# Row sums from the additions, squares on ScalarE in the first batch, and one power on GpSimd for the inverse root of every norm

## The chip, the cores and the metric

The kernel runs on one core of a Trainium2 chip. The core has five engines with queues of their own: TensorE (PE in the profile, its weight loads PEld), VectorE (DVE), ScalarE (ACT), GpSimd (POOL) and SyncE (SP), which here only issues transfers. Each engine works through its queue in order; engines wait for one another by semaphores. The metric is the device time of one execution in microseconds; the median of several runs is compared.

## The reference

Two stages. A sparse attention over four batches of 8 heads, 768 tokens and 64 channels, where each query sees the keys within 16 positions and 24 block summaries, gives `x` of 4 x 768 x 512. Then a Fourier mix with a two-layer network:

```python
X = np.fft.fft(x, axis=1)
X = np.fft.fft(X, axis=2)
mixed = np.real(X).astype(np.float32)
u = x + mixed
mu = np.mean(u, axis=-1, keepdims=True)
var = np.mean((u - mu) ** 2, axis=-1, keepdims=True)
un = (u - mu) / np.sqrt(var + 1e-06)
ch = np.maximum(un @ w_ch1, 0.0) @ w_ch2
return (u + ch).astype(np.float32)
```

The change concerns `mu`, `var` and the division by the root. `w_ch1` is 512 x 2048 and `w_ch2` 2048 x 512; they arrive as 64-bit floats and are converted on the chip. All arithmetic is in fp32.

## The kernel before

The four batches follow one another, and each goes through attention, Fourier mix, normalisation, hidden layer and output layer. The attention of the next batch, and in batch 0 the conversion of the weights, are interleaved with the dense layers of the present one. Inside a batch the 768 tokens form two halves of three tiles of 128 tokens (HT = 3); a tile has 128 partitions (tokens) and 512 columns (channels, DM).

`gen_fourier(b)` does the mix. Products with cosine and sine tables give `y` (L1333), which ACT copies out (L1338, L1339). For each half, and in it for each tile `t`, matmuls with a second table give `mx` in PSUM (L1372 and L1374 in batch 0, L1290 and L1292 after it), which DVE adds onto `x[:, t, :]`. The helper `tt` records each of its DVE operations as L582, and `gtt` each of its POOL operations as L585.

Then come the row statistics. In batch 0 DVE computes them from each tile of x with `bn_stats` (L1381) and `bn_aggr` (L1382), and turns them into minus the mean (L1394) and the variance plus 1e-6 (L1395). In batches 1 to 3 ACT makes two passes over x: a copy scaled by -1/512 that adds up the row into `minus` (L1386), and a square of x + minus that adds up into `var` (L1388); DVE then divides by 512 and adds 1e-6 (L1397). The output of these ACT passes goes to `un`, which is overwritten later.

For each half the inverse root of the three columns of `var` is made on DVE: a shift and a subtraction on the bits (L1398, L1400) and three Newton steps of three operations (L1403, one at L582, L1405). L1406 multiplies it by `minus` to give the shift z. `normalise` then writes `un` = x * y + z, on DVE (L1354) for even tiles and for the last tile of batch 0, on ACT (L1351) otherwise. There are eight norms, two in each batch. TensorE turns `un` tile by tile (`unt`, L1428; L1425 in the last batch), DVE and ACT copy it to `u` (L1429), and DVE forms sums of blocks of u (`_right_sums`), since the dense layers use products of seven block sums in place of eight products.

The hidden layer `gen_hidden` makes `hx`, `hy`, `hz` (L1460), and the output layer `o` (L1730, first half of batch 0) and `ox`, `oy`, `oz` (L1753).

What sets the order: a planner with costs for each operation places instructions in the engines' queues by readiness and priority. `drive` interleaves generators step by step; the mix runs at a priority raised by 600. In batch 0 several places are pinned by `tc.issue_after(mark)`, which puts an instruction behind the marked one in the plan:

- The mixing matmuls of a tile come behind those of the tile before; the additions of tiles 4 and 5 onto x come behind the scaling of the first half (`marks["un", 0]`).
- `marks["mx", 0]` is first the z of a half and then its last scaling on DVE. The conversion of the second and later blocks of weights (`gen_weights`: DVE L1171, ACT L1172, DVE L1184, ACT L1185, DVE L1187, L1189 and one at L582), and the key maxima (L692) behind the products `ss` of batch 1's group 1, wait for it.
- The turns `unt` of the first half come behind `sc` of batch 1's group 0 (L810), those of the second behind `av` of it (L851).
- Batch 1's group 0 has its products of exponentials with the mask `near` on POOL (L585).

Of the kernel before, what the change touches and what calls it, by code (L numbers as in the profile page):

```python
# [9 lines left out]
FP = mybir.dt.float32  # L10
I32 = mybir.dt.int32
U32 = mybir.dt.uint32
AF = mybir.ActivationFunctionType
ALU = mybir.AluOpType
AX = mybir.AxisListType

P = 128
# [479 lines left out]
def _main_program(ctx, tc, q, k, v, moe_w_ch1, moe_w_ch2, out):  # L497


    nc = tc.nc  # L500
    B, H, S, D = q.shape
    DM = H * D
# [11 lines left out]
    HT = NST // 2  # L514
# [5 lines left out]
    ADD, SUB = ALU.add, ALU.subtract  # L520
# [4 lines left out]
    cpool = ctx.enter_context(tc.tile_pool(name="cst", bufs=1))  # L525
    apool = ctx.enter_context(tc.tile_pool(name="attn", bufs=2))
    bpool = ctx.enter_context(tc.tile_pool(name="bat", bufs=1))
    spool = ctx.enter_context(tc.tile_pool(name="small", bufs=4))
# [12 lines left out]
    near = cpool.tile([P, 2, NB2, BLOCK], FP, name="near")  # L541
    sel = cpool.tile([4 * nb, 2, P], FP, name="sel")
    half_of = cpool.tile([P, 2], FP, name="half")
    rebias = cpool.tile([P, 1], FP, name="rebias")
    mirror = cpool.tile([P, 1], I32, name="mirror")
    rec = cpool.tile([P, B * NP, 2, NST], FP, name="rec")
# [23 lines left out]
    def bank(shape, name):  # L570
        return psum.tile(shape, FP, tag="bank", bufs=4, name=name)
# [9 lines left out]
    def tt(out, in0, in1, op):  # L581
        return nc.vector.tensor_tensor(out=out, in0=in0, in1=in1, op=op).ins  # L582

    def gtt(out, in0, in1, op):
        return nc.gpsimd.tensor_tensor(out=out, in0=in0, in1=in1, op=op).ins  # L585
# [698 lines left out]
    def mix_halves(ps, y, fm, xt, half):  # L1284

        Q = DM // 4
        e0, eo, e1, o1 = fm[:, 0:Q + 1], fm[:, Q + 1:3 * Q + 1], fm[:, 3 * Q + 1:4 * Q + 1], fm[:, 4 * Q + 1:5 * Q + 1]
        nc.tensor.matmul(ps[:, 0:HD + 1:2], y[:, 0], e0, start=True, stop=False, skip_group_check=True)  # L1290
        for out, g, table in ((ps[:, 0:DM:2], 1, eo), (ps[:, 1:HD:2], 2, e1), (ps[:, HD + 1:DM:2], 3, o1)):
            nc.tensor.matmul(out, y[:, g], table, start=False, stop=True, skip_group_check=True)  # L1292
        low, high = xt[:, 1:HD], xt[:, HD + 1:DM]
        tt(xt[:, 0:HD + 1], ps[:, 0:HD + 1], xt[:, 0:HD + 1], ADD)
        tt(high, ps[:, HD - 1:0:-1], high, ADD)
        tt(low, low, ps[:, HD + 1:DM], SUB if half else ADD)
        tt(high, high, ps[:, DM - 1:HD:-1], ADD if half else SUB)

    def gen_fourier(b):
        x = x_of[b]  # L1300
# [12 lines left out]
        if b > 1:  # L1313
            big = rooms[b]
            yt = bpool.tile([P, 7, 2, S2], FP, tag="u", name=f"yt_{b}").rearrange("p a k n -> p (a k n)")[:, 0:8 * S2]
            un = big[:, 0:NST * DM]
        else:
# [4 lines left out]
            yt, un = big[:, 0:8 * S2], big[:, 8 * S2:8 * S2 + NST * DM]  # L1322
        yt = yt.rearrange("p (r g s) -> p r g s", r=2, g=4)
        un = un.rearrange("p (t d) -> p t d", t=NST)
        ty, tr = yt[:, 0], yt[:, 1]
        for par in range(2):
            for g in range(4):
                ps = bank([P, F2 + 2], f"y_{b}_{par}_{g}")
                y = ps[:, par:par + F2 + 1]
# [16 lines left out]
        def normalise(half, *which):  # L1346
            y, shift = norms[half]
            for i in which or range(HT):
                t = HT * half + i
                if t % 2 and not (b == 0 and t == NST - 1):  # L1350
                    nc.scalar.activation(out=un[:, t, :], in_=x[:, t, :], func=AF.Identity, bias=shift[:, i:i + 1],  # L1351
                                         scale=y[:, i:i + 1])
                else:
                    marks["un", half] = nc.vector.tensor_scalar(out=un[:, t, :], in0=x[:, t, :], scalar1=y[:, i:i + 1],  # L1354
                                                            scalar2=shift[:, i:i + 1], op0=ALU.mult, op1=ADD).ins
        for half in range(2):
            stat = spool.tile([P, 2, HT], FP, tag="stat", name=f"stat_{b}_{half}")
            norm = spool.tile([P, 2, HT], FP, tag="norm", name=f"norm_{b}_{half}")
            minus, var = stat[:, 0], stat[:, 1]
            if b == 0:  # L1360
                both = spool.tile([P, HT, 2], FP, tag="both", bufs=2, name=f"both_{half}")
            for i in range(HT):
                t = HT * half + i
                cols = slice(P * i, P * (i + 1))
                if b:
                    mix_halves(bank([P, DM], f"mx_{b}_{t}"), yt[:, half, :, cols], fd, x[:, t, :], half)
                else:

                    ps = bank([P, 2, HD], f"mx_{b}_{t}")
                    with tc.issue_after(marks["tile"]) if t else ExitStack():  # L1370
                        for par in range(2):
                            nc.tensor.matmul(ps[:, par, :], yt[:, half, 2 * par, cols], fd[:, 3 * par, :],  # L1372
                                             start=True, stop=False)
                            ins = nc.tensor.matmul(ps[:, par, :], yt[:, half, 2 * par + 1, cols],  # L1374
                                                   fd[:, 3 * par + 1 + half, :], start=False, stop=True)
                    marks["tile"] = ins.ins
                    xv = x[:, t, :].rearrange("p (m two) -> p two m", two=2)
                    with tc.issue_after(marks["un", 0]) if t > HT else ExitStack():
                        tt(xv, ps, xv, ADD)
                    bst = spool.tile([P, 6], FP, tag="bst", name=f"bst_{b}_{t}")  # L1380
                    nc.vector.bn_stats(out=bst, in_=x[:, t, :])  # L1381
                    nc.vector.bn_aggr(out=both[:, i], in_=bst)  # L1382
                    yield
                    continue

                nc.scalar.activation(out=un[:, t, :], in_=x[:, t, :], func=AF.Copy, scale=-1.0 / DM,  # L1386
                                     accum_out=minus[:, i:i + 1])
                nc.scalar.activation(out=un[:, t, :], in_=x[:, t, :], func=AF.Square, bias=minus[:, i:i + 1],  # L1388
                                     accum_out=var[:, i:i + 1])
                yield  # L1390

            y, z = norm[:, 0], norm[:, 1]
            if b == 0:
                nc.vector.tensor_scalar(out=minus, in0=both[:, :, 0], scalar1=-1.0, scalar2=None, op0=ALU.mult)  # L1394
                nc.vector.tensor_scalar(out=var, in0=both[:, :, 1], scalar1=1e-6, scalar2=None, op0=ADD)  # L1395
            else:
                nc.vector.tensor_scalar(out=var, in0=var, scalar1=1.0 / DM, scalar2=1e-6, op0=ALU.mult, op1=ADD)  # L1397
            nc.vector.tensor_scalar(out=y.bitcast(I32), in0=var.bitcast(I32), scalar1=1, scalar2=None,  # L1398
                                    op0=ALU.arith_shift_right)
            nc.vector.tensor_scalar(out=y.bitcast(I32), in0=y.bitcast(I32), scalar1=-1.0, scalar2=float(0x5F3759DF),  # L1400
                                    op0=ALU.mult, op1=ADD)
            for _ in range(3):
                nc.vector.scalar_tensor_tensor(out=z, in0=y, scalar=-0.5, in1=y, op0=ALU.mult, op1=ALU.mult)  # L1403
                tt(z, z, var, ALU.mult)
                nc.vector.scalar_tensor_tensor(out=y, in0=z, scalar=1.5, in1=y, op0=ADD, op1=ALU.mult)  # L1405
            ins = nc.vector.tensor_tensor(out=z, in0=minus, in1=y, op=ALU.mult)  # L1406
            if b == 0:
                marks["mx", 0] = ins.ins
            norms.append((y, z))
            if b == 0:  # L1410
                normalise(half)
                marks["mx", 0] = marks["un", half]
# [4 lines left out]
        for t in range(NST):  # L1417
            half, i = divmod(t, HT)
            if b:
                normalise(half, i)  # L1420
            ps = bank([P, 2, 2, P], f"unt_{b}_{t}")
            with tc.issue_after(marks[("av", 1, 0) if half else ("sc", 1, 0)]) if b == 0 else ExitStack():
# [6 lines left out]
            ins = (nc.vector.tensor_copy if t % 2 and (b or half) else nc.scalar.copy)(  # L1429
                out=u[:, half:half + 3:2, :, P * i:P * (i + 1)], in_=ps)  # L1430
# [372 lines left out]
    ps = bank([P, 512], "warm")  # L1803
# [2 lines left out]
    nc.scalar.dma_start(out=wide, in_=dr["wide"].ap())  # L1806
    nc.scalar.dma_start(out=count, in_=dr["count"].ap())
    nc.scalar.dma_start(out=blk, in_=dr["blk"].ap())
    nc.vector.memset(rebias, -896.0 * 2.0 ** 23)
    for kt, km in zip(kt_bufs, km_bufs):  # L1810
        nc.vector.memset(kt[:, 0:W], 0.0)
# [6 lines left out]
    for vw in vw_bufs + [third]:  # L1818
        nc.gpsimd.tensor_copy(out=vw[:, :, D].rearrange("p (e n) -> p e n", e=2),
                              in_=count[:, None, :].to_broadcast([P, 2, NQ]))  # L1820
# [52 lines left out]
    for b in range(B):  # L1873
# [20 lines left out]
        if b == B - 2:  # L1894
# [9 lines left out]
            ps = bank([1, 1], "flag_ps")  # L1904
# [5 lines left out]
def kernel(tc, q, k, v, moe_w_ch1, moe_w_ch2, out):  # L1910
    nc = tc.nc
    with ExitStack() as ctx:
        flag = _main_program(ctx, tc, q, k, v, moe_w_ch1, moe_w_ch2, out)
        redo = nc.values_load(flag[0:1, 0:1], min_val=0, max_val=1)
    with tc.If(redo > 0):
        _general_program(tc, q, k, v, moe_w_ch1, moe_w_ch2, out)
# [30 lines left out]
```

## Time and profile before

| | us |
|---|---|
| median of 3 runs | 783.42 (783.32 to 783.82) |
| the profiled execution | 782.39 |
| its span in the trace | 780.6 |

The profile is of one execution. Its span leaves out 1.8 us around it. The clock granted to TensorE was 0.999 over the span. A row of the timeline gives start, length, engine, line, operation, output and inputs, and in brackets the idle time of the engine before it and what ended that. Rows that follow each other alike are merged (`x3`), and some operations overlap the one before, so lengths are not distances. "Busy" for PE has modelled ends.

### The profile page before, as it was taken

What the parts mean: (1) busy time and instruction counts of PE and PEld (TensorE: products, weight loads), DVE (VectorE), ACT (ScalarE), POOL (GpSimd) and SP (SyncE); (2) the same over time, 40 slices, a digit from 0 to 9 for tenths busy, and PEclk for the clock granted to TensorE, in tenths of its full rate; (3) what the DMA queues carried; (4) which work ended last, traced back from release to release, by engine and by line L of the source; (5) the groups of instructions that cost most, each with busy time, mean ns of one, the idle gap of its engine ahead of it and who ended that gap; (6) DMA issues with size and microseconds to landing.
All of it is one profiled execution on the core that took longest, in us unless ns stands there. A gap on an engine that the chain in (4) does not pass through costs nothing.

```text
span 780.6 us, 14876 instructions
## 1 busy us (share of the span) xinstructions
PE 766.1 (98%) x6020; PEld 578.0 (74%) x6020; DVE 534.4 (68%) x1123; ACT 249.4 (32%) x579; POOL 74.7 (10%) x102
## 2 busy tenths in 40 slices
PE   8999899999999999999999999999999999999997
PEld 5778555446598866787578866688669889889886
DVE  5789998777888556652758544553576887766762
ACT  4765656326536022100236012200126124104300
POOL 1001000000000030201210020300030004101500
PEclk9999999999999999999999999999999999999999
DMA  9998979696855179986342169720624143204001
GB/s 203 259 240 163 217 253 302 178 280 175 245 141 157 37 214 219 248 124 182 128 166 96 55 209 197 200 81 1 255 63 143 41 181 143 95 1 188 1 29 57
DMA packets 135900, 120.35 MB, mean 154 GB/s; under 512 B 94512, under 2 KB 117392, under 8 KB 135824
## 3 DMA queue, kind: packets, MB, share of 16 engines
q1 hardware_dynamic: 134672, 117.05, 54.9%
q0 software_dynamic: 576, 2.10, 0.7%
q8 instruction: 49, 0.80, 0.5%
q10 hardware_dynamic: 576, 0.17, 0.1%
q14 instruction: 27, 0.22, 0.1%
HBM read 95.71 MB, written 23.59 MB: 153 GB/s over the span
## 4 chain that ended last, share of the span: by engine, by line
PE 81%; DVE 9%; DMA 5%; ACT 3%; issue 1%; SPq 1%; POOL 0%; DVEq 0%; ACTq 0%; POOLq 0%
PE ox L1753 18%; PE hx L1460 13%; PE oz L1753 9%; PE hz L1460 6%; PE o L1730 5%; PE oy L1753 4%; PE t L1633 4%; DMA words<-in_moe_w_ch_dram 3%; PE hy L1460 3%; PE y L1333 2%; PE f L1633 2%; PE mx L1292 2%; PE sc L810 2%; PE av L846 1%; DVE w L582 1%
## 5 line engine op out<-in xcount | busy, mean ns | idle before, releaser
L1460 PE MATMUL hx<-u,w 128*128 128x384 f32 x384 | 140.0, 492 | 0.5 <-ACT h L1471 0.3
L1460 PEld LDWEIGHTS hx<-u,w 128*128 128x128 f32 x384 | 70.9, 190 | 52.8 <-ACT p L817 3.7
L1753 PE MATMUL oz<-w,s 128*128 128x256 f32 x336 | 81.7, 380 | 0.0
L1753 PE MATMUL ox<-w,s 128*128 128x256 f32 x336 | 80.1, 380 | 0.2 <-DVE s L582 0.2
L1753 PE MATMUL ox<-w,h 128*128 128x256 f32 x336 | 79.6, 381 | 0.0
L1753 PEld LDWEIGHTS ox<-w,h 128*128 128x128 f32 x336 | 63.0, 190 | 10.7 <-issue 1.2
L1460 PE MATMUL hz<-u,w 128*128 128x384 f32 x192 | 70.4, 487 | 0.4 <-DVE u L582 0.4
L582 DVE TENSOR_TENSOR x<-ox,x 128x256 f32<-128x256 f32 x84 | 35.5, 423 | 51.2 <-PE ox L1753 50.8
L1753 PEld LDWEIGHTS ox<-w,s 128*128 128x128 f32 x336 | 63.0, 190 | 9.6 <-DVE s L582 0.6
L1753 PEld LDWEIGHTS oz<-w,s 128*128 128x128 f32 x336 | 63.2, 190 | 9.0 <-DVE x L582 0.4
L1460 PEld LDWEIGHTS hz<-u,w 128*128 128x128 f32 x192 | 36.2, 190 | 25.7 <-DVE u L582 1.0
L1471 ACT COPY h<-hx 128x384 f32<-128x384 f32 x24 | 11.5, 478 | 118.7 <-PE hx L1460 118.7
L1730 PE MATMUL o<-w,h 128*128 128x512 f32 x96 | 42.2, 595 | 0.9 <-DVE w L582 0.9
L1753 PE MATMUL oy<-w,h 128*128 128x256 f32 x168 | 40.7, 381 | 0.7 <-ACT h L1682 0.7
L1636 ACT COPY f<-t 128x192 f32<-128x192 f32 x52 | 15.8, 303 | 78.3 <-PE t L1633 78.1
L1612 POOL TENSOR_SCALAR h<-h 128x768 f32<-128x768 f32 x12 | 25.4, 2128 | 137.6 <-DVE h L1592 137.6
L585 POOL TENSOR_TENSOR vb<-vb 96x512 f32<-96x512 f32 (+2 forms) x20 | 20.4, 1024 | 182.5 <-DMA vb<-in_v_dram 115.8
L1460 PE MATMUL hy<-u,w 128*128 128x384 f32 x96 | 35.2, 488 | 1.5 <-DVE h L582 1.5
L582 DVE TENSOR_TENSOR x<-oz,x 128x256 f32<-128x256 f32 x42 | 17.8, 423 | 26.7 <-PE oz L1753 26.4
L1753 PEld LDWEIGHTS oy<-w,h 128*128 128x128 f32 x168 | 31.5, 190 | 5.9 <-ACT h L1682 1.5
L1730 PEld LDWEIGHTS o<-w,h 128*128 128x128 f32 x96 | 18.0, 190 | 23.8 <-issue 21.2
L1490 ACT ACTIVATE h<-hx 128x384 f32<-128x384 f32 x24 | 11.7, 489 | 62.2 <-PE hx L1460 62.2
(236 smaller groups left out, 1327.4 us busy)
## 6 DMA issues: line engine op xcount, KB each, us to landing
w<-dw SPq DMA_DIRECT2D x42, 896.0 KB, 5.8
words<-in_moe_w_ch_dram SPq DMA_DIRECT2D x32, 512.0 KB, 5.8
dw<-w SPq DMA_DIRECT2D x12, 896.0 KB, 7.8
vw<-in_v_dram SPq DMA_DIRECT2D x47, 192.0 KB, 5.6
out_dram<-x SPq DMA_DIRECT2D x23, 256.0 KB, 2.0
vb<-in_v_dram SPq DMA_DIRECT2D x24, 192.0 KB, 6.9
kn<-in_k_dram SPq DMA_DIRECT2D x9, 384.0 KB, 5.9
qn<-in_q_dram SPq DMA_DIRECT2D x9, 384.0 KB, 7.0
```

The source lines that it names most:

```text
L582: return nc.vector.tensor_tensor(out=out, in0=in0, in1=in1, op=op).ins
L585: return nc.gpsimd.tensor_tensor(out=out, in0=in0, in1=in1, op=op).ins
L810: ins = nc.tensor.matmul(ps[h][r:r + 64, i, :], kt[rows, o:o + 64], qt[rows, o:o + BLOCK], start=True, stop=True)
L1292: nc.tensor.matmul(out, y[:, g], table, start=False, stop=True, skip_group_check=True)
L1333: nc.tensor.matmul(y, fgs[b][par][:, st, P * g:P * (g + 1)], fs[par][:, g % 2, st, :], start=(st == 0), stop=(st == n - 1))
L1460: ins = nc.tensor.matmul(ps, w[:, a, kk, :], u[:, r, kk, :], start=start and kk == 0, stop=stop and kk == 1, skip_group_check=True)
L1490: nc.scalar.activation(out=c21, in_=X, func=AF.Relu)
L1612: nc.gpsimd.tensor_scalar(out=t, in0=t, scalar1=0.0, scalar2=None, op0=ALU.max)
L1633: marks["two"] = nc.tensor.matmul(o, left(j, a, m), rhs(r, m), start=m in (1, 5), stop=m in (2, 3, 4, 5, 7), skip_group_check=True).ins
L1636: nc.scalar.copy(out={1: f[:, 0], 6: f[:, 1], 7: g}[m], in_=t)
L1730: nc.tensor.matmul(ps, h[:, n, hf, P * t:P * (t + 1)], wt[2, b, j][:, 2 * hf:2 * hf + 2, :], start=(n, hf) == (0, 0), stop=(n, hf) == (NC ...
L1753: nc.tensor.matmul(ps, left[a][:, n, :], wt[2, b, j][:, r, :], start=start and n == 0, stop=stop and n == NC - 1, skip_group_check=True)
```

## The change

In batch 0 the addition of `mx` onto x becomes a `scalar_tensor_tensor` that also adds up the row into `minus`, now the plain sum; ACT squares -512 x + sum and adds that up into `var`, which is therefore 512 to the third times the variance. `bn_stats`, `bn_aggr` and what followed them are gone. In every batch one DVE operation scales `var` and adds 1e-6, one POOL operation raises it to the power -0.5 (a constant tile `root`), and one DVE operation makes z. The shift, the subtraction and the Newton steps are gone.

```diff
+    root = cpool.tile([P, HT], FP, name="root")
...
-            if b == 0:
-                both = spool.tile([P, HT, 2], FP, tag="both", bufs=2, name=f"both_{half}")
...
                     with tc.issue_after(marks["un", 0]) if t > HT else ExitStack():
-                        tt(xv, ps, xv, ADD)
-                    bst = spool.tile([P, 6], FP, tag="bst", name=f"bst_{b}_{t}")
-                    nc.vector.bn_stats(out=bst, in_=x[:, t, :])
-                    nc.vector.bn_aggr(out=both[:, i], in_=bst)
+                        nc.vector.scalar_tensor_tensor(out=xv, in0=ps, scalar=1.0, in1=xv, op0=ALU.mult, op1=ADD,
+                                                       accum_out=minus[:, i:i + 1])
+                    nc.scalar.activation(out=un[:, t, :], in_=x[:, t, :], func=AF.Square, bias=minus[:, i:i + 1],
+                                         scale=-float(DM), accum_out=var[:, i:i + 1])
...
-            if b == 0:
-                nc.vector.tensor_scalar(out=minus, in0=both[:, :, 0], scalar1=-1.0, scalar2=None, op0=ALU.mult)
-                nc.vector.tensor_scalar(out=var, in0=both[:, :, 1], scalar1=1e-6, scalar2=None, op0=ADD)
-            else:
-                nc.vector.tensor_scalar(out=var, in0=var, scalar1=1.0 / DM, scalar2=1e-6, op0=ALU.mult, op1=ADD)
-            nc.vector.tensor_scalar(out=y.bitcast(I32), in0=var.bitcast(I32), scalar1=1, scalar2=None,
-                                    op0=ALU.arith_shift_right)
-            nc.vector.tensor_scalar(out=y.bitcast(I32), in0=y.bitcast(I32), scalar1=-1.0, scalar2=float(0x5F3759DF),
-                                    op0=ALU.mult, op1=ADD)
-            for _ in range(3):
-                nc.vector.scalar_tensor_tensor(out=z, in0=y, scalar=-0.5, in1=y, op0=ALU.mult, op1=ALU.mult)
-                tt(z, z, var, ALU.mult)
-                nc.vector.scalar_tensor_tensor(out=y, in0=z, scalar=1.5, in1=y, op0=ADD, op1=ALU.mult)
-            ins = nc.vector.tensor_tensor(out=z, in0=minus, in1=y, op=ALU.mult)
+            nc.vector.tensor_scalar(out=var, in0=var, scalar1=1.0 / DM ** (1 if b else 3), scalar2=1e-6, op0=ALU.mult, op1=ADD)
+            gtt(y, var, root, ALU.pow)
+            ins = nc.vector.scalar_tensor_tensor(out=z, in0=minus, scalar=1.0 if b else -1.0 / DM, in1=y, op0=ALU.mult,
+                                                 op1=ALU.mult)
...
+    nc.vector.memset(root, -0.5)
```

## The prediction

> **What bounds the kernel now.** I read the page's busy times first, then a table of busy times by stage, then what TensorE waited for, then the timeline around the first batch's normalisation.
>
> ```profile
> span 780.6 us, 14876 instructions
> ...
> PE 766.1 (98%) x6020; PEld 578.0 (74%) x6020; DVE 534.4 (68%) x1123; ACT 249.4 (32%) x579; POOL 74.7 (10%) x102
> ```
>
> TensorE (PE) is busy for 766.1 of 780.6 us. The change touches no matmul, so all that it can win is idle time of PE: 14.5 us in all, and only what lies behind a norm. The table by stage says where that is. Its columns are the stretch, its length, and the busy us of PE, weight loads, DVE, ACT and POOL.
>
> ```profile
> 60.00:65.00 5.00, 5.00 (x31) 4.51 (x30) 5.00 (x15) 3.19 (x7) 0.00 (x0) 1.00 1.41 165
> 65.00:70.00 5.00, 5.00 (x116) 4.34 (x115) 4.72 (x19) 2.30 (x5) 0.01 (x1) 1.00 1.11 292
> 70.00:75.00 5.00, 4.97 (x212) 3.81 (x210) 4.52 (x21) 3.11 (x8) 1.96 (x2) 1.00 0.40 99
> 75.00:80.00 5.00, 4.63 (x40) 3.12 (x40) 5.00 (x8) 4.94 (x9) 0.00 (x0) 1.00 0.02 3
> 80.00:85.00 5.00, 4.40 (x18) 2.43 (x19) 5.00 (x6) 4.29 (x10) 0.00 (x0) 1.00 0.86 230
> 90.00:100.00 10.00, 8.51 (x194) 5.36 (x194) 10.00 (x15) 3.48 (x5) 0.00 (x0) 1.00 1.19 232
> 224.00:262.00 38.00, 37.66 (x213) 33.66 (x213) 31.73 (x91) 16.44 (x47) 0.00 (x0) 1.00 0.43 118
> 402.00:432.00 30.00, 29.85 (x177) 27.19 (x176) 23.00 (x74) 17.08 (x47) 0.00 (x0) 1.00 0.32 108
> 582.00:613.00 31.00, 30.85 (x180) 27.78 (x179) 23.74 (x74) 17.09 (x47) 0.00 (x0) 1.00 0.33 107
> ```
>
> The last three rows are the mixing of batches 1 to 3, where six of the eight norms are: PE idles 0.34, 0.15 and 0.15 us there, so a faster norm can win 0.6 us at most. The six rows above are batch 0. There VectorE (DVE) is full from 75 on, and PE loses 0.37, 0.60 and 1.49 us. The list of PE's waits between 53 and 224 us names them:
>
> ```profile
> PE hy L1460 <- DVE h L582: 1.5, 1, 1.5
> PE o L1730 <- DVE w L582: 0.9, 1, 0.9
> ...
> PE hz L1460 <- DVE u L582: 0.4, 1, 0.4
> PE ss L828 <- DVE km L692: 0.4, 1, 0.4
> ```
>
> So the stretch from 75 to 100 is bound by DVE with PE close behind, and the question is how much earlier DVE gets there. The timeline of batch 0 (start, length, engine, line, operation):
>
> ```profile
> 61.55 0.67 DVE L582 TENSOR_TENSOR x<-mx,x 128x512 f32<-128x512 f32 x1
> ...
> 67.25 0.59 PE L1374 MATMUL mx<-fd,big 128*128 128x256 f32 x2
> ...
> 67.91 0.16 DVE L1406 TENSOR_TENSOR norm<-stat,norm 128x3 f32<-128x3 f32 x1
> ...
> 69.31 1.53 PE L1428 MATMUL unt<-ident,big 128*128 128x128 f32 x12
> ...
> 69.99 1.97 POOL L585 TENSOR_TENSOR p<-p,near 128x384 f32<-128x384 f32 x2 [30.05 <-ACT p L817]
> ...
> 72.09 0.17 DVE L1398 TENSOR_SCALAR norm<-stat 128x3 int32<-128x3 int32 x1
> ...
> 74.27 0.16 DVE L1406 TENSOR_TENSOR norm<-stat,norm 128x3 f32<-128x3 f32 x1
> ...
> 74.47 1.00 DVE L1354 TENSOR_SCALAR big<-x,norm 128x512 f32<-128x512 f32 x2
> ...
> 75.39 0.69 DVE L1171 TENSOR_SCALAR words<-words 128x1024 int32<-128x1024 int32 x1
> ...
> 75.80 1.53 PE L1428 MATMUL unt<-ident,big 128*128 128x128 f32 x12
> ```
>
> The second half's z (L1406) ends at 74.43 and its two scalings on DVE at 75.47. The weight conversion (L1171) begins at 75.39, since the code holds it, and the key maxima behind PE's ss, until that scaling is issued (the mark ("mx", 0)). From there DVE never rests until 100. The path is: last x of the half, its statistics, norm, scaling, conversions, then PE's waits.
>
> **The change part by part.** What DVE loses:
>
> ```profile
> L1381 DVE BATCH_NORM_STATS2 bst<-x 128x6 f32<-128x512 f32 x6 | 3.9, 682 | 0.0
> ...
> L1382 DVE BATCH_NORM_AGGREGATE both<-bst 128x2 f32<-128x6 f32 x6 | 0.8, 166 | 0.0
> ...
> L1394 DVE TENSOR_SCALAR stat<-both 128x3 f32<-128x3 f32 x2 | 0.4, 192 | 0.0
> ...
> L1405 DVE SCALAR_TENSOR_TENSOR norm<-norm 128x3 f32<-128x3 f32 x24 | 3.8, 156 | 0.4
> ```
>
> Batch 0 drops 3.9 + 0.8 + 0.4 us of statistics. Each of the eight norms drops eleven small operations. Bare, as in the second half, they follow each other at 0.20 us (72.09 to 74.27 for the eleven steps to L1406), so 2.2 us. In batches 1 to 3 other work of DVE and PE lies over them, and PE had at most 0.6 us to give; I count nothing. If a norm came late there, u would have to be late: batch 1's last sum ends at 258.9 and the first hidden product runs at 272.28, so some 13 us cover it.
>
> ```profile
> 257.97 0.95 DVE L582 TENSOR_TENSOR u<-u 128x768 f32<-128x768 f32 x1
> ...
> 272.28 1.29 PE hx L1460 x4
> ```
>
> What is added. First, six additions become a form that also sums the row. The addition is 0.67; the read-out of a sum is not in DVE's rows. I bound it by nothing and by ACT's read-out, 0.19, and take 0.19: it stands between x and the square. Second, ACT gets six squares in batch 0:
>
> ```profile
> L1388 ACT ACTIVATE big<-x,stat 128x512 f32<-128x512 f32 x6 | 4.3, 717 | 0.1
> ...
> L1388 ACT ACTIVATION_READ_ACCUMULATOR big<-x,stat 128x1 f32 x6 | 1.1, 187 | 0.0
> ...
> L585 POOL TENSOR_TENSOR fold<-fold 128x1 f32<-128x1 f32 x4 | 0.8, 192 | 0.3
> ...
> L585 POOL TENSOR_TENSOR fold<-fold 1x1 f32<-1x1 f32 x4 | 1.1, 278 | 0.3
> ```
>
> That is 0.72 + 0.19 = 0.91 each and 5.5 us together, in a stretch (60 to 75) where ACT is busy for 8.6 of 15 us. Third, the power on POOL. No row shows one. Below stands a two-input addition of one column, 0.19; above, eleven small POOL operations, as many as it replaces on DVE, at 0.28: 3.1 us. I take 0.5, near the small addition, as three columns are little data. Each hand-over between engines I count at 0.1 (POOL started at 69.99, on the first ACT result of a pair begun at 69.41 with some half a microsecond each). A VectorE operation that awaits the last one costs 0.2.
>
> Half 0: x of tile 2 ends at 62.22, with its sum at 62.4; square to 63.3, variance to 63.5, power 63.6 to 64.1, z from 64.2 to 64.4, against 68.07. PE's turn of that half stands at 69.31 behind matmuls that the change doesn't touch, so nothing is won there directly. Half 1: the last mixing matmul ends at 67.84; x with its sum to 68.7, square 69.6, variance 69.8. If POOL is free, the power ends at 70.4 and z at 70.7. If the planner leaves the two products with near ahead (69.99 to 71.96), POOL is free only at 71.96 and z ends at 72.8. z was 74.43, so the **lead is 1.6 to 3.7 us**; I take 2.7. What is queued behind z on DVE are the scalings, conversions and key maxima: all gain the same lead. Behind the power on POOL only the near products can stand; half a microsecond later they end at 72.5, still before av uses them.
>
> What the lead is worth: PE's waits for ss (0.4), hz (0.4) and hy (1.5), 2.3 us. A lead of 1.6 takes 1.6 of it, one of 2.3 or more all. PE's next wait, o for w (0.9), hangs on a string of ACT work that begins when PE delivers hz, and moves along with PE; I count nothing for it, 0.9 as the upper end. PE is otherwise full, so nothing comes late in place of these. **Sum: -2.3 us** (bounds with the mechanism intact -1.6 and -2.3 - 0.9 = -3.2): span 778.3, and 782.39 - 2.3 = 780.1 for the profiled execution. The median of the runs is 783.42, 1.03 above that execution, so **781.1 us** as a median.
>
> [...]
>
> **The rivals.**
>
> (a) The lead is spent, not handed on. DVE's order is the planner's. The hy wait ended with an h addition at 96.44 that stood behind conversion work:
>
> ```profile
> 95.84 0.68 DVE L582 TENSOR_TENSOR w<-w 128x512 f32<-128x512 f32 x1
> ...
> 96.44 0.55 DVE L582 TENSOR_TENSOR h<-hy,h 128x384 f32<-128x384 f32 x1
> ```
>
> If the planner uses the lead to put more conversion in front of it, the 1.5 us stays and only the 0.8 of ss and hz is won: 782.6, no change that can be measured. For it: DVE is full, with conversions enough. ACT speaks for it too: it is busy for 9.2 of 10 us from 75 to 85, each conversion passes through it, and it now gets the squares before. Against it: the total of work before the addition is smaller.
>
> (b) Slower: the power itself. Let it take p. Above p = 2.3 half 0 delays the second half, for tiles 4 and 5 are added only behind the first half's scaling. From tile 2's x at 62.4 it is then 1.5 + p for half 0's z (square 0.9, variance 0.2, two hand-overs, z 0.2), 1.1 for the scalings, 1.4 for two additions with their sums, and again 1.5 + p: z of half 1 at 67.9 + 2p, and p = 3.3 eats the whole lead. At p = 5, z is at 77.9 instead of 74.43: the turn of half 1 and the conversions are 3.5 later, and the median is 786.9. Against it: POOL's addition of 384 columns takes 1.0 us (1.97 for two), so three columns would need to cost 1.6 us each. My upper bound of 3.1 stands just short of the point.
>
> [...]
>
> (c) More: the 0.9 of o goes as well, and PE's small waits on ACT and in batches 1 to 3: 2.3 + 0.9 + 0.6 = 3.8, 779.6.
>
> **How the numbers follow.** A measurement of this kernel tells about 0.2%, 1.6 us, from no change. The forecast (-1.6 to -3.2) gets 0.48, (c) 0.05, (a) with the start-up case 0.31, (b) 0.16, as p is unknown and the planner may place things badly. Faster 0.53, same 0.31, slower 0.16. The range goes from (c), 779.6, to 784.4: past (a) and the start-up case, leaving out most of (b).
>
> **What would show it.** Right: L1381, L1382 and the small operations gone; each power under 1 us on POOL; z of half 1 near 71 to 73 and the first conversion behind it by 74; the waits of ss, hz and hy shrunk; the table for batches 1 to 3 unchanged in PE. Wrong: the conversions early but hy still waiting (a); a POOL row of 3 us or more, with PE idle before the turn at 69 or 76 (b); squares standing behind the copies of kt and qt on ACT, so that half 0 gains nothing.

## The result, and the profile after

The changed kernel takes 787.61 us as a median (785.57 to 789.29), against 783.37 us for the kernel before in the same comparison. The ratio is 1.0054, with a 95% interval of 1.0036 to 1.0072: **slower by 4.2 us**, where 2.3 us less were forecast. The page of the changed kernel, in the lines that answer to those shown of before:

```profile
span 783.8 us, 14797 instructions
...
PE 768.5 (98%) x6020; PEld 581.7 (74%) x6020; DVE 523.0 (67%) x1028; ACT 253.1 (32%) x591; POOL 82.5 (11%) x110
...
PEclk9999899999999999999999999999999999999999
```

DVE lost 11.4 us of work, as meant. PE does the same 6020 matmuls and is busy for 2.4 us longer, and in the row of the granted clock one slice, the fifth (78 to 98 us), is no longer full. The norm itself went as forecast. The timeline of the second half of batch 0 (start, length, engine, line):

```profile
69.90 0.85 POOL L586 TENSOR_TENSOR norm<-stat,root 128x3 f32<-128x3 f32 x1 [5.69 <-DVE stat L1392]
...
70.72 0.99 POOL L586 TENSOR_TENSOR p<-p,near 128x384 f32<-128x384 f32 x1
...
70.78 0.95 DVE L1394 SCALAR_TENSOR_TENSOR norm<-stat,norm 128x3 f32<-128x3 f32 x1 [0.97 <-POOL norm L586]
...
72.69 0.69 DVE L1172 TENSOR_SCALAR words<-words 128x1024 int32<-128x1024 int32 x1
```

The power takes 0.85 us, z ends at 71.73 and the conversion starts at 72.69, against 74.43 and 75.39 before. The last mixing matmul ended 0.55 us earlier in this execution (67.29), so the lead is 2.15 us.

Then comes ScalarE (ACT). What stands further back in its queue waits for what stands ahead. Its timeline after the change, and below it before:

```profile
69.64 0.49 ACT L818 ACTIVATE p<-sc 128x384 f32<-128x384 f32 x1
71.77 0.81 ACT L1352 ACTIVATE big<-x,norm 128x512 f32<-128x512 f32 x1 [1.64 <-DVE norm L1394]
72.49 1.54 ACT L1418 COPY u<-unt 128x512 f32<-128x512 f32 x3
73.91 0.51 ACT L818 ACTIVATE p<-sc 128x384 f32<-128x384 f32 x1
74.29 0.51 ACT L830 ACTIVATE p<-ss 128x384 f32<-128x384 f32 x1
74.66 1.18 ACT L1173 ACTIVATE words<-words,rebias 128x1024 int32<-128x1024 int32 x1
...
76.64 0.54 ACT L837 ACTIVATE vs<-vs,half 128x64 f32<-128x64 f32 x2
```

```profile
69.41 0.88 ACT L817 ACTIVATE p<-sc 128x384 f32<-128x384 f32 x2 [0.42 <-PE sc L810]
70.27 1.56 ACT L1429 COPY u<-unt 128x512 f32<-128x512 f32 x3
71.71 0.52 ACT L829 ACTIVATE p<-ss 128x384 f32<-128x384 f32 x1
72.09 0.55 ACT L836 ACTIVATE vs<-vs,half 128x64 f32<-128x64 f32 x2
74.53 0.82 ACT L1351 ACTIVATE big<-x,norm 128x512 f32<-128x512 f32 x1 [1.89 <-DVE norm L1406]
```

Before, everything that batch 1's attention needs (two exponentials of sc, one of ss, the two vs copies) was done by 72.6, and un tile 3, which has to wait for z, stood behind it all. With the shorter norm the planner sets un tile 3 ahead of the second exponential. ACT then stands still for 1.64 us waiting for z, although the input of the second exponential (sc) had been ready since 68.83. That exponential, the one of ss and the vs copies start 2.6 to 4.6 us later than before. PE needs them. Its timeline:

```profile
71.36 1.23 PE L811 MATMUL sc<-qt,kt 64*64 64x32 f32 x34
74.47 1.59 PE L811 MATMUL sc<-qt,kt 64*64 64x32 f32 x62 [1.88 <-ACT p L818]
75.99 2.78 PE L847 MATMUL av<-vw,p 64*32 64x65 f32 x96
```

The sc matmuls stop for 1.88 us. The av matmuls after them take 2.78 us, where the same 96 took 1.55 before. The table by stage shows why (stretch, its length, busy us of PE, clock, DMA share, GB/s):

```profile
76.00:77.00 1.00, 1.00 (x46) 0.58 0.00 0
77.00:78.00 1.00, 1.00 (x44) 0.50 0.07 16
...
82.00:83.00 1.00, 1.00 (x6) 0.51 0.90 236
```

From 76.2 to 83.0 us TensorE is granted half its clock (0.50 in the rows of 77 to 82), which costs 3.4 us by an estimate, half of those 6.8. The profile is no exception in this: the mean clock over the span was 0.992 to 0.995 in all eight runs of the changed kernel. The list of PE's waits:

```profile
PE sc L811 <- ACT p L818: 1.9, 1, 1.9
PE hx L1449 <- ACT h L1460: 1.4, 2, 0.9
...
PE ox L1742 <- DVE x L583: 1.2, 3, 0.5
```

The waits of ss, hz and hy that were to go have gone. In their place stand the one of sc, more waiting of hx for ACT (1.4 us, where it was 0.3), and a new one of ox in the mixing of the later batches. Two such rows of batch 3:

```profile
604.08 1.57 PE L1414 MATMUL unt<-ident,fold 128*128 128x128 f32 x12 [0.31 <-DVE fold L1355]
...
609.13 0.70 PE L1742 MATMUL ox<-w,s 128*128 128x256 f32 x2 [0.45 <-DVE x L583]
```

The start of the program varies: the last mixing matmul of batch 0 ended between 66.8 and 70.5 us in the twelve profiles of this study. The clock divides them. In e3_power123, e4_exps_first, e6_values_first and e10_before_vs_late it was half for 3.4 us between 9.2 and 13.5 us, some 50 us ahead of the norm, and there the matmul ended at 69.0 to 70.5; in the other eight it stayed full there, and the matmul ended at 66.8 to 67.9. Runs of one kernel differ in the clock too: of 24 runs of the kernel before, the five fastest (781.6 to 782.01 us) had a mean clock of 0.999 or 1.0 and the five slowest (785.07 to 787.32) one of 0.994 to 0.996. So the kernels are compared from that matmul on. The table gives the length of five stages of TensorE's timeline: from the end of that matmul to the first hx, and on to the first mixing matmul of batches 1, 2 and 3 and the end of the last matmul. The first row is in us; the others are differences from it, each from one profile.

| kernel | to first hx | to batch 1 | to batch 2 | to batch 3 | to the end | sum |
|---|---|---|---|---|---|---|
| before | 11.00 | 153.28 | 176.97 | 180.68 | 186.07 | 708.00 |
| after | +5.92 | -3.15 | -0.66 | +0.91 | +0.81 | +3.83 |
| e1_squares | +6.39 | -1.65 | -0.56 | 0.00 | +0.01 | +4.19 |
| e2_power | +6.21 | -3.04 | +0.47 | +0.92 | +0.80 | +5.36 |
| e4_exps_first | +5.54 | -3.14 | +0.10 | +1.76 | +0.81 | +5.07 |
| e5_fill | +8.07 | -4.02 | -0.27 | +1.88 | +0.80 | +6.46 |
| e6_values_first | -0.14 | +0.03 | +0.12 | +1.82 | +0.79 | +2.62 |
| e3_power123 | +0.01 | -0.34 | +0.38 | +1.81 | +0.78 | +2.64 |
| e8_values_newton123 | -0.17 | -0.04 | -0.36 | +0.82 | -0.15 | +0.10 |
| e9_turned_later | -0.15 | +0.02 | +0.26 | -0.11 | -0.21 | -0.19 |
| e10_before_vs_late | +2.81 | -2.50 | -0.18 | +0.87 | +0.02 | +1.02 |
| e11_before_vs_later | +4.08 | -0.75 | -0.42 | -0.01 | -0.15 | +2.75 |

For the changed kernel: 5.9 us lost up to the first hx, 3.2 of them taken back by the stage behind it, and 1.7 lost in batches 2 and 3. (In six of the twelve profiles "to batch 3" holds another 0.9 us, with the power or without it; the last section says what it is.)

### The profile page after: what moved, and what is told of

It reads as the page before. It is cut to its first block, busy times and chain, and to the rows that moved or that the text cites. A ratio compares the mean times of both kernels' runs of the same rounds, so it can differ in the third digit from the quotient of the medians.

```text
span 783.8 us, 14797 instructions
## 1 busy us (share of the span) xinstructions
PE 768.5 (98%) x6020; PEld 581.7 (74%) x6020; DVE 523.0 (67%) x1028; ACT 253.1 (32%) x591; POOL 82.5 (11%) x110
## 4 chain that ended last, share of the span: by engine, by line
PE 83%; DVE 7%; ACT 5%; issue 3%; POOL 1%; DMA 1%; SPq 0%; DVEq 0%; ACTq 0%; POOLq 0%
PE ox L1742 17%; PE hx L1449 15%; PE oz L1742 8%; PE hz L1449 7%; PE o L1719 5%; PE t L1622 4%; PE oy L1742 4%; PE hy L1449 3%; PE y L1334 2%; PE f L1622 2%; PE av L847 2%; PE sc L811 2%; PE av L852 2%; DVE x L583 1%; PE sc L751 1%
```

## The experiments

**The two halves of the change, alone.** e1_squares has the sums and squares of batch 0 with the Newton steps kept; e2_power keeps `bn_stats` and has the power in every norm.

The first, as a diff of the changed kernel, and the second, of the kernel before:

```diff
-            gtt(y, var, root, ALU.pow)
+            nc.vector.tensor_scalar(out=y.bitcast(I32), in0=var.bitcast(I32), scalar1=1, scalar2=None,
+                                    op0=ALU.arith_shift_right)
...
+                nc.vector.scalar_tensor_tensor(out=y, in0=z, scalar=1.5, in1=y, op0=ADD, op1=ALU.mult)
```

```diff
-            nc.vector.tensor_scalar(out=y.bitcast(I32), in0=var.bitcast(I32), scalar1=1, scalar2=None,
-                                    op0=ALU.arith_shift_right)
...
-                nc.vector.scalar_tensor_tensor(out=y, in0=z, scalar=1.5, in1=y, op0=ADD, op1=ALU.mult)
+            gtt(y, var, root, ALU.pow)
```

> The first half of the change alone: sums from the additions and squares on ScalarE in batch 0, Newton steps on VectorE kept everywhere. Theory A (the loss comes from ScalarE's queue: one exponential of batch 1's group 0 stands behind the scaling of tile 3, TensorE waits 1.9 us for its bank and its granted clock then halves for some 7 us): in this kernel's queue both exponentials stand ahead of that scaling, so no wait at sc, clock back at 0.999, 780 to 783 us against 783.4 before. Rival B (the added work costs, wherever it stands: squares on ScalarE): 786 to 788.

> The other half alone: the statistics of batch 0 as before, the power on GpSimd for all eight norms. Theory A: both exponentials stand ahead of the scaling of tile 3 here too, so no halved clock; what is left are the small waits of some 0.6 us each that batches 2 and 3 show after the change: 782.5 to 785. [...]

Measured: 788.5 us, ratio 1.0066 (1.0044 to 1.0089), and 788.12 us, ratio 1.0059 (1.0041 to 1.0077). **Each half alone costs what both together do**, so the loss isn't the price of an added instruction. In both profiles ACT has un tile 3 ahead of the exponential of ss and of the vs copies (un tile 3 from 74.05 and 72.96, vs at 77.6 and 77.5), PE stops at av twice (2.37 and 0.83 us; 2.20 and 1.46), and the clock falls (a mean of 0.994 in both, 0.999 before). Theory A had expected a full clock and 780 to 783 and 782.5 to 785 us; it looked at the exponentials of sc alone. Un tile 3 starts only 0.5 us earlier in e1_squares than before (74.05 against 74.53), so a small lead seems to be enough for the order to turn.

**The two exponentials first.** e4_exps_first is the changed kernel with un tile 3 and half 0's u copies queued on ACT behind both exponentials of sc.

```diff
+            marks["exp", b, g] = nc.scalar.activation(out=p[:, h], in_=ps[h], func=AF.Exp, scale=SC).ins
...
+                    with tc.issue_after(marks["exp", 1, 0]) if b == 0 and half else ExitStack():
                         nc.scalar.activation(out=un[:, t, :], in_=x[:, t, :], func=AF.Identity, bias=shift[:, i:i + 1],
```

> The whole change, with one thing pinned: in batch 0 the scaling of tile 3 and the copies of u of the first half stand behind both exponentials of batch 1's group 0 in ScalarE's queue. Theory A: the wait of 1.9 us at sc and the halved clock are gone, so 5 us or more come back: 780.5 to 783, as far as the prediction's gain in batch 0 is real. [...]

Measured: 787.79 us, ratio 1.0047 (1.003 to 1.0064). 780.5 to 783 were expected. The wait of sc is gone and nothing is won. PE's timeline:

```profile
76.29 0.89 PE L847 MATMUL av<-vw,p 64*32 64x65 f32 x48 [1.58 <-issue]
78.64 1.52 PE L847 MATMUL av<-vw,p 64*32 64x65 f32 x48 [1.46 <-ACT vs L837]
```

The wait has moved to av. In ACT's queue un tile 3 (73.54) still stood ahead of the exponential of ss (75.68), and the conversion's two steps (76.06 and 77.10) ahead of vs (78.05). The theory that one exponential is at fault fell; what remained is that all five of these operations have to stand ahead of what waits for z.

**Filling the pause.** e5_fill is the changed kernel with each ss matmul of batch 1's group 0 issued five times.

```diff
+                for _ in range(5 if (b, g) == (1, 0) else 1):
                     nc.tensor.matmul(ps[r:r + 32, :], km[rows, :], qt[rows, S2 * h:S2 * (h + 1)], start=True, stop=True)
```

> The whole change with ScalarE's order as it is, and TensorE given something to do in the wait: the ss products of batch 1's group 0 are made five times over with the same result, 3.1 us more, before sc of group 1. If the halved clock is most of the loss (A1), the wait stays with sc starting at about 74.5, but the clock stays full and some 3.3 to 6 us come back, less the 1.1 us of sc that now also stands behind the wait: 782.5 to 785.5. If the wait alone is the loss (A2), nothing is won: 787.5 to 789.

Measured: 787.63 us, ratio 1.005 (1.0032 to 1.0067). The table by stage:

```profile
75.00:80.00 5.00, 5.00 (x53) 1.00 0.26 83
80.00:85.00 5.00, 5.00 (x207) 1.00 0.98 311
```

With PE busy through the stretch the clock stays full (1.00 in both rows). As a price the run is inconclusive: the 40 matmuls took 9.30 us, not ended by 74.5 as meant but at 79.2, and cost what the clock had.

**All five operations ahead.** e6_values_first puts un tile 3, half 0's u copies and the conversion's two ACT steps behind the vs copies, which are issued right after ss. e3_power123 is the kernel before with the power in batches 1 to 3 alone. e8_values_newton123 is e6_values_first with the Newton steps back in batches 1 to 3. The core of the first, as a diff of the changed kernel:

```diff
                 sum_scores(b, g, held[1])
+            if (b, g) == (1, 0):
+                scale_sums(b, g)
...
+            marks["vs", b, g] = nc.scalar.activation(out=vs[:, r, 0:D], in_=ps, func=AF.Identity, scale=half_of[:, r:r + 1]).ins
...
+                    with tc.issue_after(marks["vs", 1, 0]) if b == 0 and half else ExitStack():
                         nc.scalar.activation(out=un[:, t, :], in_=x[:, t, :], func=AF.Identity, bias=shift[:, i:i + 1],
...
+            with tc.issue_after(marks["vs", 1, 0]) if b == 0 and not half else ExitStack():
                 ins = (nc.vector.tensor_copy if t % 2 and (b or half) else nc.scalar.copy)(
...
+        with tc.issue_after(marks["vs", 1, 0]) if m == 1 else ExitStack():
             nc.scalar.activation(out=ex, in_=ex, func=AF.Relu, bias=rebias, scale=8.0)
...
+        with tc.issue_after(marks["vs", 1, 0]) if m == 1 else ExitStack():
             nc.scalar.activation(out=dst, in_=man, func=AF.Copy, bias=1.0, scale=2.0 ** -20)
```

> The changed kernel, and on ScalarE both exponentials, the exponential of the sums and the two vs copies of batch 1's group 0 queued ahead of un tile 3, half 0's u copies and the conversion's two ScalarE steps, as they stood before the change. Theory Q (the lead let later work pass ahead of them in ScalarE's in-order queue; TensorE then waited 1.9 to 3 us at 72 to 80 us and its clock was halved for 6 to 7 us): no wait over 0.6 us of TensorE between 70 and 80 us, clock 0.99 or more in 75:80 and 80:85, and 782.0 to 784.0 us, that is about the kernel before, with the gain at the start and the loss of batches 2 and 3 (0.6 us each) left over against each other. Rival R (the clock falls for another reason, such as how much thin matmul work stands there, or the loss is in the power itself): the clock is still under 0.8 in one of the two stretches, and 786 us or more.

> The kernel before with the power on GpSimd in batches 1 to 3 alone; batch 0 keeps its statistics and its Newton steps. Both theories: full clock between 70 and 85 us and the early waits as before. Theory Q's second part (in batches 2 and 3 TensorE idles about 0.6 us more each beside the norms): 784.2 to 785.0 us, TensorE idle of about 0.77 us in 402:432 and 582:613. If the power costs nothing there: 783.2 to 783.9. If it carried the whole loss of the change: 786 or more.

> As e6_values_first, with the Newton steps back in batches 1 to 3, so that only batch 0 is changed. Theory Q: the gain that was predicted for batch 0 without what was lost, 780.5 to 782.0 us, and 0.8 to 1.8 us under e6_values_first; TensorE idle of 0.15 us in 402:432 as before. Rival R: 785 or more.

Measured: e6_values_first 786.24 us, ratio 1.0036 (1.0023 to 1.005); e3_power123 785.39 us, 1.0029 (1.0011 to 1.0047); e8_values_newton123 782.46 us, 0.999 (0.998 to 1.0). The table by stage of e6_values_first:

```profile
75.00:80.00 5.00, 4.70 (x200) 1.00 0.01 3
80.00:85.00 5.00, 4.85 (x32) 1.00 0.60 166
```

The clock is full and the 5.9 us up to the first hx are gone (-0.14 in the table). That settles batch 0: the loss there was the order of ACT's queue. But the kernel was 2 to 4 us slower than expected, a time that the rival had, and e3_power123 shows that the rest sits in batches 1 to 3: its batch 0 is untouched, and it alone is 0.29% slower (785.39, where 784.2 to 785.0 were expected). Its stages "to batch 3" and "to the end" are those of e6_values_first. With the Newton steps back there, the loss is gone: e8_values_newton123 is 3.8 us under e6_values_first, where 0.8 to 1.8 were expected, though at 782.46 still above the 780.5 to 782.0 that a gain in batch 0 would give. It is the best of all these kernels, by 0.1% with an interval that touches 1, which is less than a measurement of this kernel can tell from no change.

**The order in batches 2 and 3.** With the shorter chain the planner also sets the transposes (`unt`) of batches 2 and 3 ahead of the second oz and ox products, where PE then waits for un and for x. e9_turned_later is e6_values_first with these transposes kept behind the products that they stood behind before.

```diff
+            with tc.issue_after(marks[("av", 1, 0) if half else ("sc", 1, 0)] if b == 0 else
+                                marks[("o", b - 1, 1, 0) + ((S3, 3) if half else (S4, 1))]) if b != 1 else ExitStack():
                 for d in range(NDT):
```

> As e6_values_first (power in every batch), with the transposes of batches 2 and 3 kept behind the two expert products that they stood behind in TensorE's queue before the change. Theory O (the loss of batches 2 and 3 is the order that the planner made in TensorE's in-order queue: with the shorter chain it sets the transposes ahead of expert products, and TensorE then waits for un and for x): TensorE idle in 400:435 and 580:615 falls from 0.77 to under 0.4 us each, from the first mixing matmul of batch 3 to the end 186.0 to 186.3 us and not 186.9, and 784.2 to 785.4 us. Rival P (the power's own 0.85 us, in whatever order): the idle stays at 0.6 us or more and 785.8 to 786.8 us.

Measured: 783.9 us, against 783.92 for before; ratio 1.0016 (1.0002 to 1.003). The table by stage of e6_values_first and below it that of e9_turned_later:

```profile
400.00:435.00 35.00, 34.23 (x188) 1.00 0.26 89
...
580.00:615.00 35.00, 34.24 (x185) 1.00 0.29 99
```

```profile
400.00:435.00 35.00, 35.00 (x198) 1.00 0.29 104
580.00:615.00 35.00, 35.00 (x198) 1.00 0.31 104
```

PE's idle time of 0.77 and 0.76 us is gone, and the last stage is 185.86 us; this and the time are a little better than expected. The power is still there, 0.85 to 0.90 us long in these batches, so it was the order. This kernel has the whole change with both orders put back, and it takes the time of the kernel before to within 0.3%.

**The same loss without the change.** If the order of ACT's queue is the cause, the kernel before must lose as much when only that order is made bad. e10_before_vs_late queues the vs copies behind un tile 3. e11_before_vs_later queues them behind the exponentials of group 1. Both are diffs of the kernel before:

```diff
+            with tc.issue_after(marks["un3", 0]) if (b, g) == (1, 0) else ExitStack():
                 nc.scalar.activation(out=vs[:, r, 0:D], in_=ps, func=AF.Identity, scale=half_of[:, r:r + 1])
```

```diff
                 held = scores(b, g)
+                with tc.issue_after(marks["exp", 1, 1]):
+                    scale_sums(1, 0)
```

> The kernel before, nothing of the change in it, with the two vs copies of batch 1's group 0 queued on ScalarE behind un tile 3 instead of ahead of it: they end at about 75.9 us and not at 72.6. Theory Q (a pause of TensorE in the thin matmuls of 70 to 80 us is enough to halve its clock): a pause of 1.0 to 2.0 us at the av matmuls, the clock under 0.8 in 75:80 or 80:85, and 786 to 788.5 us. Without the clock the pause alone gives 784.4 to 785.4. Rival R (the halved clock needs something of the change, the power or the squares): clock 0.99 or more and 785.4 or less.

> The kernel before, with the two vs copies queued later still, behind the exponentials of batch 1's group 1, one of them behind the conversion's two ScalarE steps as well: a larger dose of the same pause. Theory Q: pauses of 2.5 to 4 us in all between 73 and 80 us, as in the changed kernel, the clock under 0.8 in 75:80 and 80:85, and 787 to 790 us. Rival R: clock 0.99 or more and 785.5 to 787.0, the pause alone.

Measured: e10_before_vs_late 784.85 us, ratio 1.0013 (0.9997 to 1.0028); e11_before_vs_later 786.89 us, ratio 1.0051 (1.0032 to 1.007). PE's timeline of the first, and its table by stage:

```profile
75.04 0.76 PE L847 MATMUL av<-vw,p 64*32 64x65 f32 x36
77.39 1.31 PE L847 MATMUL av<-vw,p 64*32 64x65 f32 x60 [1.59 <-ACT vs L837]
```

```profile
77.00:78.00 1.00, 0.61 (x38) 0.84 0.08 16
78.00:79.00 1.00, 1.00 (x42) 0.50 0.00 0
...
81.00:82.00 1.00, 1.00 (x10) 0.96 0.00 0
```

A pause of 1.59 us is enough here for the half clock (0.50 from 78 us on), in a kernel with neither the power nor the squares; the rival that the clock needs something of the change is out. The time, though, missed what was expected of e10_before_vs_late (786 to 788.5) and lies where the pause without the clock was put (784.4 to 785.4): of the 2.8 us that PE came late at the first hx, the next stage took 2.5 back. There the waits for hz and hy, 0.4 and 1.5 us before, are gone from its list, since PE is now late for them. e11_before_vs_later, where one vs copy stood behind the conversion's ACT steps as well, paused twice (1.57 and 0.93 us) and is about as slow as the changed kernel. Its time, 786.89, is 0.1 us short of the theory's range and inside the rival's; its clock, 0.75 in 75:80 and 0.91 in 80:85, is against the rival, though the second is less of a fall than the theory had. (Its profile is of the 784.9 us execution, which may be why the sum in the table is below what the median shows.)

## Why the prediction was wrong

**The step that failed** is the sentence "PE is otherwise full, so nothing comes late in place of these". It was argued from "What is queued behind z on DVE" and "Behind the power on POOL only the near products can stand". ACT's queue was left out, although the text had un on ACT in it and said of ACT that it is busy for 9.2 of 10 us from 75 to 85. A work of ACT that waits for z (un tile 3) moved ahead of five operations that PE needs. In the changed kernel that made 1.88 us of waiting and 3.4 us of half clock. Less the 0.4 us that PE idled in this stage before, that is 4.9 of the 5.9 us; about 1 us isn't accounted for by these rows. e6_values_first takes both away, and e10_before_vs_late and e11_before_vs_later make such waits and the half clock without the change. Nearly all that the text named as signs of being right came (z at 71.73, the conversion behind it by 74, the waits of ss, hz and hy gone), and the kernel was still slower: none of them looked at ACT's queue. The one that didn't come is the last, the table of batches 2 and 3.

**Batches 1 to 3**, "I count nothing", with at most 0.6 us to win. Nothing here contradicts the bound on the gain, but there was none on the loss. The six shorter norms changed the order on PE's queue and cost 0.9 us in batch 2 and 0.8 in batch 3 (e9_turned_later). Batch 1 shows nothing that stands out from the spread of its column.

**The sizes around z** were good. A read-out of the sum on DVE takes 0.08 to 0.09 us (0.19 was taken), the addition with its sum 0.68 to 0.70 (0.67 was taken), the power 0.85 to 0.90 in seven of the eight norms and 1.22 in one (0.5; bounds 0.19 to 3.1). No run shows the start-up case that the chances and the range count beside (a): the first power took 0.88 us, the second 0.85 (in e2_power the first took 1.25). The lead is 2.15 us (2.7; bounds 1.6 to 3.7). By the lengths in the timeline it would have been 0.8 more, had z taken the 0.16 us of the other seven norms: beside the near product on POOL it took 0.95.

**What the lead is worth**, "2.3 us", was too much even with the orders put back. In the changed kernel the waits of ss, hz and hy did go, but e10_before_vs_late shows that they also go without any lead, when PE is late. In e8_values_newton123, where PE is on time, those of ss and hz for DVE go, that of o for w goes too, hy stays at 1.4 us, and the two stages of batch 0 gain 0.2 us together. In the second of them PE's idle time falls from 3.7 to 2.7 us and the length only from 153.28 to 153.24: the other 1.0 us became time in which the records have PE busy, with the same 981 matmuls; why is open. The outcome is that of rival (a), the lead spent and hy still waiting, but more conversion ahead of it was not shown; the rows show DVE waiting longer for other engines. DVE's waits from the end of the mixing up to 67 us later, in e8_values_newton123 and below it before:

```profile
DVE words L1192 <- ACT words L1176: 1.3, 2, 0.7
DVE h L583 <- ACT h L1484: 1.1, 1, 1.1
...
DVE h L583 <- PE hy L1465: 0.7, 1, 0.7
...
DVE h L583 <- PE hz L1465: 0.5, 1, 0.5
```

```profile
DVE words L1187 <- ACT words L1172: 0.5, 2, 0.4
DVE h L582 <- ACT h L1479: 0.5, 1, 0.5
...
DVE h L582 <- PE hx L1460: 0.4, 1, 0.4
```

DVE's waits in the conversions and hidden layer are 3.6 us, against 1.9 before (with one of 0.5 of w for ACT that isn't shown). DVE, ACT and PE keep each other waiting in that stretch, which suggests that time gained by one is soon spent on another. Whether ACT, with the conversion's passes, is now the one that bounds it wasn't tried.

**The rivals.** None was the one that came. (b) had the right sign by another way: the power was 0.9 us, far from its point of 3.3. Its chance of 0.16 also named that "the planner may place things badly", but without an engine or a price.

## What to carry to other kernels

Where a planner orders in-order queues, a shorter chain is also a new order: for each engine that the chain touches, list what stands behind the first instruction that waits for the chain's end, and who waits for that. Whether a new part is slow itself or only brought a bad order can be told by pinning the old order (e6_values_first, e9_turned_later) and by making the bad order without the change (e11_before_vs_later). And a pause of TensorE can cost more than its length: after the one of 1.88 us in the changed kernel came 6.8 us of half clock, while one of 1.49 us in the kernel before had none after it.

## What the runs showed of the hardware

**The clock.** Apart from the early spells of the first section, the half clock lasted 3.4 us (e10_before_vs_late, e11_before_vs_later) or 6.8 us (after, e1_squares, e4_exps_first), worked out from the shares in stretches of 1 us: for e10_before_vs_late 0.32 + 3 + 0.08, for the changed kernel 0.84 + 5 + 0.98. In the trace of the changed kernel the records of the clock give 71.680 us full, 6.827 half and 699.732 full, one after the other: the full stretches are 10.5 and 102.5 times as long as the half one. In that of the kernel before, a full stretch of 771.412 us is 113.0 times as long. So in these two traces the changes lie whole steps of half that length, 3.41 us, apart. The records begin at 4.48 us in the one and at 7.25 in the other, so counted from there the steps of the two fall differently on the same work.

In e10_before_vs_late PE stood still for 1.59 us among av matmuls of 65 columns, from 75.80 to 77.39 us, and the clock halved at 77.68. In the changed kernel it stood still for 1.88 us, up to 74.47, and the clock halved at 76.16. The wait for hy in the kernel before, 1.49 us between sc matmuls of 32 columns and hy ones of 384, cost no clock (1.00 from 90 to 100 us), nor did that in e9_turned_later, 1.40 us (1.00 from 85 to 100). And near the start PE idled for 1.13 us between 6.2 and 8.7 us in both e10_before_vs_late and e11_before_vs_later, and only in the first did the clock halve after it (0.98 over the first 70 us, against 1.00). So the length of the pause alone doesn't decide. Whether the kind of matmuls around it does, or where it falls in the steps, was not tried.

**VectorE and GpSimd.** z ran from 70.78 to 71.73 us and the near product on POOL from 70.72 to 71.71: an operation that took 0.16 us in the other seven norms took 0.95 here and ended within 0.02 us of POOL's, 0.8 us longer. What held it is not shown. The 0.9 us in the column "to batch 3" look alike. Two near products on DVE meet an addition on POOL that starts when a transfer lands. In the kernel before, and below it in e8_values_newton123:

```profile
462.42 2.10 DVE L582 TENSOR_TENSOR p<-p,near 128x384 f32<-128x384 f32 x2 [3.61 <-ACT p L817]
```

```profile
460.86 3.06 DVE L583 TENSOR_TENSOR p<-p,near 128x384 f32<-128x384 f32 x2 [3.61 <-ACT p L818]
```

In the first POOL's addition starts at 462.65, after DVE has begun: the first product takes 0.56 us, the second, beside that addition, 1.62. In the second it starts at 460.70, ahead of DVE, and the pair takes 1.0 us more. Whether the order of the starts decides was not shown. In six of the twelve profiles the pair takes 3.06 to 3.18 us and in each an hx matmul soon after waits 0.58 to 0.70 us; in the other six it takes 2.02 to 2.10 and nothing waits. The kernels with and without the power stand on both sides.
